# A new hand-written order and a split last copy in an attention and cosine FFN kernel

## The chip, the cores and the metric

The kernel runs on one core of a Trainium2 chip. The metric is the device time of one execution, in microseconds (us); the time of a kernel is the median of several runs.

## The reference

The first half is linear attention with random features on 64 heads (8 batches of 8 heads, 576 positions, 64 values each); its result is laid out as 4608 tokens of 512 values. The second half is a feed-forward layer with 2048 hidden values.

```python
def phi(x):
    proj = np.einsum('bhsd,df->bhsf', x, w_phi)
    proj = proj - np.max(np.abs(proj), axis=-1, keepdims=True)
    return np.concatenate([np.exp(proj), np.exp(-proj)], axis=-1)
q_p, k_p = phi(q), phi(k)
kv = np.einsum('bhsf,bhsd->bhfd', k_p, v)
z = np.sum(k_p, axis=2)
num = np.einsum('bhsf,bhfd->bhsd', q_p, kv)
den = np.einsum('bhsf,bhf->bhs', q_p, z)[..., None] + 1e-06
x = (num / den).transpose(0, 2, 1, 3).reshape(4608, 512)
h = x @ w_in
out = (h * np.cos(h)) @ w_out
```

## The kernel before

The kernel is a list of 3778 steps. Each step (`Step`) belongs to one engine (PE = TensorE, ACT = ScalarE, DVE = VectorE, POOL = GpSimd, SP = the queue that issues the DMAs), holds the function that issues its instructions, and names the steps that it depends on and the buffers that it takes or uses. The functions `attention(u)`, `convert`, `reload` and `visit(v)` make the steps; `plan()` then only walks through the table `ORDER`, a list of all step numbers, and calls each step's function. So `ORDER` sets the order of the instructions on every engine and on SP's queue, and each engine works strictly in that order. `plan()` also gives each buffer of the ring "bank" (the eight PSUM banks) the bank whose last user stands earliest in the table; so a new order gives other banks too. The rings of buffers in SBUF have the sizes in `rings`: three for "eq", two for "o", three each for the weights "wi" and "wo", two for "v".

**Attention.** There are 32 units of two heads each. A unit loads q and k (`load`) and v (`load_v`); PE projects q (`q_mm`, `q_end`) and k (`k_mm`, `k_end`); for the first units PE also subtracts the maximum (`k_sub`). ACT makes the exponentials (`exp_k`, `exp_q`). PE forms the product of keys and values (`kv_mm`: from unit 8 on one step of 72 matmuls, L705 and L711), ACT copies it (`kv_out`), and PE applies the queries (`x_mm`, two steps with 72 matmuls in all, L740 and L746). DVE divides and transposes, and SP stores the unit's result to `xs` in memory. The matmuls of `kv_mm` and `x_mm` have 65 or 130 columns.

**Feed-forward.** The tokens are worked in batches of 512 (`c`), each split into visits (`v`, the list `course`) that go through pairs of weight tiles. The first nine visits (stage "m.") take plain products of 512 columns (`mm1`, L960); the later ones (stage "n.") use a Strassen-like scheme with seven products of six 256-column matmuls each (`mm1`, L912), between which ACT copies partial sums (`snap`, L924) and DVE adds (`even`, `odd`). Then follow cosine and splitting into a high and a low part on ACT and DVE, and the second product, `mm2` (six matmuls of 512 columns, L1009 to L1011; a step `one` is half of it), which adds into four banks `acc`. The weights are converted once (`convert`) and stored in a second form; from the later visits on they are loaded again (`reload`, L516: `wi` 1792 KB, `wo` 1024 KB).

**The end of a visit.** `out_copy` copies the four banks to SBUF: tb 0 and 2 on ACT (L1056), tb 1 and 3 on DVE (L1058), or it adds the earlier partial sum (L1049); `out_store` stores them. The last visit but one is the batch of tail rows (c = 8); its store makes four DMAs for each copy (L1065). In the last visit the copies go to buffers of the ring "eq", which attention no longer needs.

The steps that the text names: 315 and 316 `exp_q`, 321 and 322 `x_mm` of unit 7; 408 `load_v` and 436 `kv_mm` of unit 10; 943 and 1216 `kv_mm` of units 23 and 30; 1554 the last `mm2` of a visit of stage "m.", 1559 and 1561 two of its copies, 1560 and 1562 their stores; 3494, 3498, 3500, 3496 the copies of the tail batch; 3543 to 3546 the first four steps `one` of the last visit; 3650 and 3651 products of that visit; 3776 the last copy, 3777 its store.

Of the kernel before, what the change touches and what calls it, by code (L numbers as in the profile page):

```python
# [25 lines left out]
def phi_attention_then_cos_ffn(ctx: ExitStack, tc: tile.TileContext, qkT, vS, w_phi, w_in, w_out, out):  # L26
# [5 lines left out]
    DM, FF = w_in.shape  # L32
# [35 lines left out]
    class Step:  # L68
# [1073 lines left out]
```

## Time and profile before

| | |
|---|---|
| median of 3 runs | 1047.81 us |
| the runs | 1048.76, 1045.80, 1047.81 us |
| the profiled execution | 1045.83 us |
| its span (first to last instruction) | 1044.1 us |
| what lies around the span | 1.7 us |
| mean granted TensorE clock | 0.998 of 2.4 GHz |

The profile is of one execution. PE is TensorE's matmuls, PEld its weight loads. The ends of matmuls are modelled, so distances are best taken from start to start.

### The profile page before, as it was taken

The numbers are of one execution on the slowest core, as the hardware profiler recorded it, in microseconds if no ns is written. First come the engines' busy times: TensorE is split into PE (matmuls) and PEld (weight loads), VectorE is DVE, ScalarE is ACT, GpSimd is POOL, SyncE is SP. The second block draws the span as 40 slices with busy tenths as digits, with TensorE's granted clock in tenths as the row PEclk, the third lists the DMA queues.
The fourth block names the chain that finished last, engine by engine and source line by source line (L and its number), as shares of the span: only waits on it lengthen the run. The fifth ranks groups of instructions, "written<-read, shape, count | busy, mean of one in ns | idle before, by whom it ended". The sixth has DMA issues, their size and how long they took to land.

```text
span 1044.1 us, 24213 instructions
## 1 busy us (share of the span) xinstructions
PE 1029.5 (99%) x9738; PEld 883.2 (85%) x9738; DVE 744.7 (71%) x1426; ACT 797.6 (76%) x1639; POOL 147.9 (14%) x231
## 2 busy tenths in 40 slices
PE   9998999999999999999999999999999999999998
PEld 6777788888878878888888898989888999898896
DVE  7999898999798877765776467666566465555444
ACT  6989999888887799785788869895887664455443
POOL 3453322201102001301122010211011000000000
PEclk9999999999999999999999999999999999999999
DMA  7576566267556836795427662585435755652852
GB/s 247 178 238 210 161 192 210 85 232 284 173 198 208 284 106 213 245 313 213 161 86 283 202 240 78 171 315 178 160 97 192 255 164 179 245 197 80 277 201 81
DMA packets 88768, 204.44 MB, mean 196 GB/s; under 512 B 20688, under 2 KB 42320, under 8 KB 84816
## 3 DMA queue, kind: packets, MB, share of 16 engines
q1 hardware_dynamic: 88512, 202.83, 57.4%
q8 instruction: 76, 1.25, 0.5%
q14 instruction: 36, 0.29, 0.1%
q10 hardware_dynamic: 144, 0.07, 0.0%
HBM read 154.63 MB, written 48.23 MB: 194 GB/s over the span
## 4 chain that ended last, share of the span: by engine, by line
PE 87%; DMA 6%; DVE 4%; ACT 1%; issue 1%; SPq 0%; DVEq 0%; ACTq 0%
PE bank L912 23%; PE bank L1009 12%; PE bank L1010 12%; PE bank L1011 12%; PE bank L960 10%; PE bank L740 5%; PE bank L705 5%; PE bank L555 3%; PE bank L601 3%; DMA wi_parts<-wi 2%; PE bank L711 1%; DMA wi<-wi_parts 1%; DMA qk<-qkT 1%; PE bank L647 1%; DMA x_raw<-xs 1%
## 5 line engine op out<-in xcount | busy, mean ns | idle before, releaser
L1009 PE MATMUL bank<-wo,gh 128*128 128x512 f32 x576 | 229.1, 398 | 1.1 <-DMA out<-o 0.8
L1010 PE MATMUL bank<-wo,gh 128*128 128x512 f32 x576 | 225.6, 392 | 0.2 <-DVE wo L462 0.2
L1011 PE MATMUL bank<-wo,gl 128*128 128x512 f32 x576 | 224.5, 390 | 0.0
L986 DVE SCALAR_TENSOR_TENSOR g<-g,hs 128x512 f32<-128x512 int32 x144 | 98.5, 691 | 69.2 <-ACT g L982 60.4
L594 POOL TENSOR_TENSOR pq<-pq,bq 128x288 f32<-128x288 f32 x128 | 111.7, 903 | 184.2 <-DVE bq L590 133.3
L924 ACT ACTIVATE hs<-bank 128x256 f32<-128x256 f32 x192 | 71.5, 385 | 86.0 <-PE bank L912 80.7
L659 ACT ACTIVATE ek<-bank,mk 128x128 f32<-128x128 f32 x464 | 128.4, 410 | 3.2 <-DVE mk L642 2.9
L1009 PEld LDWEIGHTS bank<-wo,gh 128*128 128x128 f32 x576 | 108.5, 188 | 24.9 <-issue 2.8
L1011 PEld LDWEIGHTS bank<-wo,gl 128*128 128x128 f32 x576 | 108.2, 188 | 23.7
L49 ACT ACTIVATE gh<-g 128x512 fp32r<-128x512 f32 x144 | 90.9, 637 | 48.4 <-DVE g L993 25.9
L993 DVE TENSOR_TENSOR g<-hs,g 128x512 f32<-128x512 f32 x144 | 99.5, 696 | 38.0 <-ACT g L990 37.5
L54 DVE TENSOR_TENSOR gl<-g,gh 128x512 fp32r<-128x512 f32 x144 | 99.2, 691 | 37.6 <-ACT gh L49 36.2
L912 PE MATMUL bank<-xh_t,wi 128*128 128x256 f32 x768 | 124.4, 284 | 0.0
L1010 PEld LDWEIGHTS bank<-wo,gh 128*128 128x128 f32 x576 | 108.6, 189 | 18.1 <-DVE wo L462 0.7
L990 ACT ACTIVATE g<-g,halfpi 128x512 f32<-128x512 f32 x144 | 101.3, 718 | 23.0 <-DVE g L986 22.4
L912 PEld LDWEIGHTS bank<-xh_t,wi 128*128 128x128 f32 x768 | 109.5, 191 | 7.5 <-ACT hs L924 0.8
L586 POOL COPY m<-m 32x36 f32<-32x36 f32 x96 | 35.5, 369 | 464.5 <-DVE m L581 461.8
L912 PE MATMUL bank<-xh_b,wi 128*128 128x256 f32 x576 | 93.0, 284 | 0.0
L912 PEld LDWEIGHTS bank<-xh_b,wi 128*128 128x128 f32 x576 | 82.4, 191 | 5.4 <-DVE xt L771 0.8
L665 ACT ACTIVATE eq<-pq 128x576 f32<-128x576 f32 x128 | 81.3, 708 | 4.0 <-PE bank L746 2.2
L912 PE MATMUL bank<-xl_t,wi 128*128 128x256 f32 x384 | 77.3, 283 | 0.0
L740 PEld LDWEIGHTS bank<-kv,eq 128*64 128x64 f32 x2048 | 65.5, 139 | 11.2 <-ACT eq L665 3.7
(91 smaller groups left out, 1809.5 us busy)
## 6 DMA issues: line engine op xcount, KB each, us to landing
wi<-wi_parts SPq DMA_DIRECT2D x30, 1792.0 KB, 8.0
wo<-wo_parts SPq DMA_DIRECT2D x30, 1024.0 KB, 5.6
qk<-qkT SPq DMA_DIRECT2D x31, 640.0 KB, 4.8
x_raw<-xs SPq DMA_DIRECT2D x47, 256.0 KB, 4.8
vs<-vS SPq DMA_DIRECT2D x32, 325.0 KB, 4.7
wi_raw<-w_in SPq DMA_DIRECT2D x8, 1024.0 KB, 6.8
wo_raw<-w_out SPq DMA_DIRECT2D x8, 1024.0 KB, 6.7
xs<-xt SPq DMA_DIRECT2D x128, 64.0 KB, 4.5
```

Source lines behind the costliest of these rows:

```text
L54: eng.tensor_tensor(out=out, in0=in_, in1=hi.bitcast(F32), op=ALU.subtract)
L594: qeng.tensor_tensor(out=d["pq"][:, c], in0=d["pq"][:, c], in1=d["bq"][:, c], op=ALU.subtract)
L659: ACT.activation(out=e[:, g, s * P:(s + 1) * P], in_=pk[:, g, :], func=AF.Exp, scale=1.0 - 2.0 * s, bias=d["lk" if s == 0 else "mk", i][:, ...
L740: PE.matmul(out=ps[64 * h:64 * h + 64, 65 * g:65 * g + 65], lhsT=d["eq", j][:, n, c:c + 64], rhs=d["kv"][:, 2 * n + j, :], start=h not in ...
L912: PE.matmul(out=out, lhsT=w[:, part, block, j * P:(j + 1) * P], rhs=d[x, name][:, j * HC:(j + 1) * HC], start=start and k == 0, stop=k == ...
L960: PE.matmul(out=bank(b), lhsT=w[:, part, 2 * r + kt // 2, kt % 2 * P:(kt % 2 + 1) * P], rhs=d.get(("from", kt), d)[x, kt], start=(k == 0), ...
L986: DVE.scalar_tensor_tensor(out=g, in0=g.bitcast(I32), scalar=-TWO_PI, in1=m["hs", r], op0=ALU.mult, op1=ALU.add)
L990: ACT.activation(out=n["g"], in_=n["g"], func=AF.Sin, bias=halfpi, scale=1.0)
L993: DVE.tensor_tensor(out=n["g"], in0=m["hs", r], in1=n["g"], op=ALU.mult)
L1009: PE.matmul(out=a, lhsT=gh[:, t], rhs=w[:, 0, r], start=first, stop=False)
L1010: PE.matmul(out=a, lhsT=gh[:, t], rhs=w[:, 1, r], start=False, stop=False)
L1011: PE.matmul(out=a, lhsT=gl[:, t], rhs=w[:, 0, r], start=False, stop=last)
```

## The change

The table `ORDER` is replaced as a whole; it has one entry more (3779), because the last copy is now two steps. Before the change, TensorE passes from one kind of matmul to another 468 times along the table (grouping `kv_mm` with `x_mm`, `q_end` with `k_end`, and all 512-column steps of the feed-forward part), after it 419 times. The set of steps is otherwise the same. ACT loads its tables of functions 76 times along the old order and 70 times along the new one.

The copy of the last bank (tb = 3 of the last visit, step 3776) goes to a buffer of the ring "o" in place of "eq"; ACT copies its first 256 columns and a new step on DVE (`half_copy`, 3777) the other 256; the store (now 3778) waits for both.

The diff, with the table cut to the lines that hold the steps named above (old lines first):

```diff
     ORDER = [
...
-        1533, 397, 524, 411, 1523, 1569, 1534, 1542, 379, 1326, 361, 425, 1566, 381, 408, 427, 360, 1293, 383,
...
-        462, 1576, 422, 1562, 447, 448, 434, 421, 464, 366, 466, 436, 450, 1329, 451, 1330, 1555, 400, 1577,
...
-        943, 965, 908, 909, 2476, 2501, 2486, 910, 2525, 911, 2505, 2524, 2477, 2527, 2487, 2450, 2530, 944,
...
-        1232, 1179, 1244, 1231, 1234, 1216, 1233, 3001, 1235, 2991, 1181, 1236, 1182, 3040, 1183, 1246, 3013,
...
-        3598, 3573, 3620, 3581, 3599, 3622, 3545, 3500, 3600, 3617, 3574, 3625, 3621, 3546, 3575, 3609, 3496,
...
-        3766, 3767, 3770, 3768, 3772, 3771, 3769, 3774, 3775, 3773, 3776, 3777,
...
+        316, 285, 339, 1316, 315, 1541, 1317, 392, 1318, 370, 1319, 1522, 371, 372, 321, 389, 446, 391, 1523,
...
+        1576, 462, 1561, 450, 502, 451, 466, 1562, 449, 1586, 408, 1577, 328, 467, 418, 366, 1578, 452, 1555,
+        421, 454, 1332, 1344, 400, 1557, 524, 419, 367, 1587, 464, 420, 399, 1311, 453, 422, 436, 507, 1333,
...
+        909, 967, 2475, 943, 966, 973, 2476, 968, 2505, 2486, 2477, 2447, 2506, 944, 954, 2525, 874, 2526, 2448,
...
+        3038, 3021, 2991, 1146, 3022, 1179, 2992, 3023, 1216, 3043, 1233, 3024, 1247, 1181, 3003, 1235, 2993,
...
+        3593, 3580, 3499, 3543, 3597, 3599, 3581, 3544, 3600, 3617, 3601, 3545, 3574, 3546, 3575, 3553, 3582,
...
+        3765, 3759, 3766, 3767, 3770, 3768, 3772, 3771, 3769, 3774, 3773, 3776, 3775, 3777, 3778,
     ]
...
-                if v == len(course) - 1:
+                if v == len(course) - 1 and tb < NB3 - 1:
                     o = d["o", tb] = new("eq", [P, 2, S], F32, "o_last")[:, 0, 0:DM]
                 else:
                     o = d["o", tb] = new("o", [P, DM], F32, "o")
-                if tb % 2 == 0:
+                if v == len(course) - 1 and tb == NB3 - 1:
+                    ACT.activation(out=o[:, 0:HC], in_=bank(acc[tb])[:, 0:HC], func=AF.Copy, scale=1.0)
+                elif tb % 2 == 0:
                     ACT.activation(out=o, in_=bank(acc[tb]), func=AF.Copy, scale=1.0)
                 else:
                     DVE.tensor_copy(out=o, in_=bank(acc[tb]))
...
-            o = Buf("o" if v < len(course) - 1 else "eq")
-            eng = "ACT" if fresh and tb % 2 == 0 else "DVE"
+            def half_copy(tb=tb):
+                DVE.tensor_copy(out=d["o", tb][:, HC:DM], in_=bank(acc[tb])[:, HC:DM])
+
+            very_last = v == len(course) - 1 and tb == NB3 - 1
+            o = Buf("o" if v < len(course) - 1 or very_last else "eq")
+            eng = "ACT" if fresh and tb % 2 == 0 or very_last else "DVE"
...
-            cp = Step(eng, 0.5 if eng == "ACT" else 0.61, out_copy, [done[tb] if v == len(course) - 1 else before] + old, take=[] if old else [o],
+            cp = Step(eng, (0.27 if very_last else 0.5) if eng == "ACT" else 0.61, out_copy, [done[tb] if v == len(course) - 1 else before] + old, take=[] if old else [o],
                       use=[acc[tb]] + ([o] if old else []), kind=stage + "out_copy")
-            partial[c, tb] = Step("SP", 0.36 if c < TAIL else 1.5, out_store, [cp], use=[o], kind=stage + "out_store", pipe=0.75)
+            cps = [cp]
+            if very_last:
+                cps.append(Step("DVE", 0.34, half_copy, [done[tb]], use=[acc[tb], o], kind=stage + "out_copy"))
+            partial[c, tb] = Step("SP", 0.36 if c < TAIL else 1.5, out_store, cps, use=[o], kind=stage + "out_store", pipe=0.75)
```

## Rows read from the trace of the kernel before

**Rows 1.** The page's first part: busy us (share of the span) xinstructions of each engine.

```profile
PE 1029.5 (99%) x9738; PEld 883.2 (85%) x9738; DVE 744.7 (71%) x1426; ACT 797.6 (76%) x1639; POOL 147.9 (14%) x231
```

**Rows 2.** Busy time by stretch; behind the engines: granted clock, DMA share, GB/s.

```profile
93.00:97.00 4.00, 1.49 (x10) 0.50 (x8) 3.90 (x10) 3.97 (x6) 0.92 (x4) 1.00 0.95 298
97.00:101.00 4.00, 3.80 (x70) 3.68 (x70) 3.90 (x10) 4.00 (x14) 0.21 (x1) 0.61 0.86 307
101.00:112.00 11.00, 10.29 (x180) 8.26 (x179) 10.70 (x21) 11.00 (x27) 5.37 (x10) 0.99 0.73 193
...
566.00:573.00 7.00, 5.94 (x152) 5.43 (x152) 4.11 (x12) 5.26 (x13) 3.07 (x4) 1.00 1.02 397
573.00:779.00 206.00, 206.00 (x2037) 181.53 (x2037) 128.14 (x269) 165.59 (x365) 25.37 (x42) 1.00 0.52 176
779.00:785.00 6.00, 4.41 (x131) 4.04 (x127) 5.74 (x17) 5.94 (x10) 0.62 (x3) 1.00 0.99 354
...
971.00:976.00 5.00, 4.23 (x30) 3.76 (x29) 2.97 (x6) 2.71 (x6) 0.00 (x0) 1.00 0.53 143
...
1039.60:1044.10 4.50, 0.00 (x0) 0.00 (x0) 0.69 (x1) 0.00 (x0) 0.00 (x0) 0.92 0.49 186
```

**Rows 3.** Who PE waited for: us in total, times, longest.

```profile
PE bank L711 <- issue: 2.6, 2, 1.6
```

**Rows 4.** Timeline of PE around 1020 us: start, duration, engine, line.

```profile
1020.23 0.64 PE L912 MATMUL bank<-xh_b,wi 128*128 128x256 f32 x4
...
1020.95 0.40 PE L1009 MATMUL bank<-wo,gh 128*128 128x512 f32 x1
...
1022.34 0.39 PE L1009 MATMUL bank<-wo,gh 128*128 128x512 f32 x1
...
1023.70 0.64 PE L912 MATMUL bank<-xh_t,wi 128*128 128x256 f32 x4
...
1024.41 0.40 PE L1009 MATMUL bank<-wo,gh 128*128 128x512 f32 x1
```

**Rows 5.** Timeline of PE, 780 to 785 us.

```profile
782.36 0.61 PE L711 MATMUL bank<-vs,ek 128*64 128x130 f32 x7
784.55 0.33 PE L711 MATMUL bank<-vs,ek 128*64 128x130 f32 x1 [1.59 <-issue]
```

**Rows 6.** The page's DMA queues: packets, MB, share of 16 engines.

```profile
q8 instruction: 76, 1.25, 0.5%
```

**Rows 7.** Busy time and counts from the start to each of the two waits.

```profile
0.00:570.45 570.45, 563.77 (x5827) 467.69 (x5827) 471.02 (x902) 488.11 (x987) 118.81 (x182) 1.00 0.61 205
0.00:782.70 782.70, 774.97 (x7991) 653.99 (x7991) 604.70 (x1183) 658.22 (x1359) 144.54 (x226) 1.00 0.59 199
```

**Rows 8.** Timeline, 965 to 975 us, the end of the tail batch.

```profile
965.45 0.58 ACT L1056 ACTIVATE o<-bank 128x512 f32<-128x512 f32 x1
966.05 7.21 SPq L1065 DMA_DIRECT2D out<-o  x8
...
973.76 0.69 DVE L1058 COPY o<-bank 128x512 f32<-128x512 f32 x1 [1.94 <-DMA out<-o]
...
974.50 0.50 PE L1009 MATMUL bank<-wo,gh 128*128 128x512 f32 x1 [0.77 <-DMA out<-o]
```

**Rows 9.** Timeline behind 1038 us.

```profile
1039.17 0.39 PE L1011 MATMUL bank<-wo,gl 128*128 128x512 f32 x1
...
1040.33 0.69 DVE L1058 COPY o_last<-bank 128x512 f32<-128x512 f32 x1 [1.40 <-DMA out<-o_last]
```

**Rows 10.** Groups by line: count, busy us, mean ns, idle before.

```profile
L924 ACT ACTIVATE hs<-bank 128x256 f32<-128x256 f32 x192 | 71.5, 385 | 86.0 <-PE bank L912 80.7 <-DVE g L993 4.2
...
L943 DVE TENSOR_TENSOR hs<-bank,hs 128x256 f32<-128x256 f32 x48 | 20.1, 419 | 55.0 <-PE bank L912 53.4 <-ACT hs L924 1.4
```

**Rows 11.** Weight loads of L516: from issue to landing.

```profile
DMA to landing us min/median/max: 4.8/7.6/11.5
```

**Rows 12.** The page's DMA issues: queue, count, KB each, median us from issue to landing.

```profile
vs<-vS SPq DMA_DIRECT2D x32, 325.0 KB, 4.7
```

409 rows, old and new, of the table ORDER are left out of this document.

## The prediction

> **What bounds the kernel now.** I read the page's busy line first [rows 1], then the busy time of every engine stretch by stretch [rows 2], then who made TensorE (PE) wait [rows 3], and last the timeline at each place where PE stood idle. The busy line shows PE at 99%: 1029.5 of 1044.1 us, so 14.6 us of idle PE is about all that a better order can win, beside what PE loses while it is busy. The stretches show where that idle time lies. From 185 us on the other engines are no limit (in 573 to 779 us ScalarE (ACT) has 165.6 and VectorE (DVE) 128.1 busy of 206), and PE is idle in only a few places: 1.06 us in 566 to 573, 1.59 in 779 to 785, 0.77 in 971 to 976, and 4.5 us behind the last matmul [rows 2]. Before that, in 93 to 112 us, it is idle 2.51 + 0.20 + 0.71 = 3.4 us, and there ACT is busy 3.97 of 4, 4.00 of 4 and 11.00 of 11: ACT sets the pace, not the order of PE. In 97 to 101 us the granted clock is 0.61, that is, part of it went at the lower level (1.2 GHz), after the 2.5 us without matmuls. As matmul ends are modelled, I take PE's costs from start to start, not from its busy time.
>
> **Width changes.** Along the table PE goes from 256-column products (mm1 of the later visits, L912) to 512-column matmuls (mm2, one) 107 times before and 81 times after; all changes among matmul kinds fall from 468 to 419, but those that are not between 256 and 512 columns are 246 in both. A step of six 512-column matmuls lasts 1022.34 - 1020.95 = 1.39 us behind a product and 1023.70 - 1022.34 = 1.36 behind its own kind; a product lasts 1020.95 - 1020.23 = 0.72 behind a product and 1024.41 - 1023.70 = 0.71 behind a 512 step [rows 4]. So 26 fewer entries at 0.03 save 0.8 us, and 23 fewer returns at 0.01 give 0.2 back: **-0.5 us** (between 0 and -0.8, the rows being round to 0.01). The other 246 changes I take at nothing, since their number stays.
>
> **The two waits inside attention's last matmuls.** Both stand at L711, in kv_mm of units 23 and 30 (steps 943, 1216), and are put down to "issue": 2.6 us in two [rows 3]. From start to start the second costs more than its idle time: a run of seven started at 782.36, and the eighth came at 784.55 instead of about 782.75, some 1.8 us late [rows 5]; the first, 1.06 idle, I put at 1.3 in the same way, so 3.1 together. Nothing in the data flow was late there, but instructions were: the instruction queue brought 76 packets with 1.25 MB [rows 6], that is 16.4 KB each, and PE's 2 x 9738 instructions [rows 1] are 256 to a packet. The two waits come in front of matmul 5827 and 7991 [rows 7]; the 4328 instructions between are 17 x 256 less 24, and PE's stream holds event instructions too, which no count here includes. Both fell in a run of 144 matmuls (x_mm, x_mm, kv_mm back to back), which passes 256 instructions in under 4 us, and while the DMA engines were full (share 1.02 and 0.99, against 0.52 in between) [rows 2]. So a packet comes late where a long run of short matmuls, a packet's border and a big weight load meet. The new table breaks the run of step 943 (in front of it stand 512- and 256-column steps and k_mm) and keeps that of step 1216. Runs of 128 matmuls and more are 18 before and 17 after; counted with the border where it fell before, no run after 185 us in the new one ends on a border with a weight load just ahead, but a dozen more or fewer event instructions would put one there. I take -3.1 plus 0.7 for a new one: **-2.4 us** (between -3.1 and 0). The Trainium skill ("Runtime: NRT & Kernel Launch", Instruction fetch mechanics) says that PE is refilled in 16 KiB blocks of 256 instructions, as the packets here show, and that crossing a border is mostly hidden; these two waits disagree. By that rule alone the waits would be something else and stay, and the sum would be 2.4 us smaller (rival 2).
>
> **The end of the tail batch.** The visit before the last stores its result in pieces: step 3494's copy starts at 965.45, eight stores take SP's queue from 966.05 on, the third copy (3500) waits 1.94 us for a buffer and starts at 973.76, and PE's first matmul into that copy's bank (step 3546) at 974.50, held 0.77 us [rows 8]. From copy to that matmul it is 974.50 - 965.45 = 9.05 us. In the old table only 6.4 us of PE work stood between steps 3543 and 3546. In the new one 3546 takes another bank; the banks of the two late copies go to products 3650 and 3651, and between 3543 (now the first behind 3494's copy) and 3650 stand four "one" steps (half an mm2 each), five products and three mm2: 4 x 0.68 + 5 x 0.72 + 3 x 1.37 = 10.4 us, over 9.05. **-0.8 us** (between 0 and -1.0).
>
> **The last copy.** The last matmul starts at 1039.17 and its bank could be read at about 1039.6, but the copy starts at 1040.33, after 1.40 us, because its buffer ("eq", three of them) must first be stored by the first of the four stores [rows 9]; it ends at 1041.02, and the store, SP's last issue and the end follow (4.5 us without PE in all). In the new kernel the buffer is one of ring "o", last used by the visit before, so nothing holds it. No row shows ScalarE and VectorE reading one bank at once; the nearest are 128x256 reads of a bank alone, 0.385 us on ACT and 0.419 on DVE [rows 10]. Side by side the copy ends at 1039.6 + 0.42 = 1040.0, one after the other at 1040.4: **-1.0 us** (between -0.6 and -1.0; I take the first, as the two steps name no wait on each other). The Trainium skill ("PSUM — Partial Sum Buffer", PSUM bank collisions raise a hardware error) wants two engines kept apart on one bank, reads included; with such a wait added the gain would be the 0.6.
>
> **The early stretch.** In front of the first x_mm of unit 7 (steps 321 and 322), where PE waited longest, ACT has the same 96 steps ahead of exp_q 315 in both tables, and PE 97 steps in both, of which two differ. With ACT full [rows 2], that wait stays: **0** (gain up to 3.4 us idle and 1 us of slow clock, loss up to 1). One load moves the wrong way: v of unit 10 (step 408) stood ahead of the two partial stores 1560 and 1562 in SP's queue and now stands behind them, so it waits for their copies, and the stores, weight load and x loads queued behind it wait as well. Cover: 10.3 us of PE work stand between the last mm2 ahead of these copies (step 1554) and kv_mm of unit 10 (436); the load takes 4.7 us [rows 12], the copy some 0.7 of its own and what is queued on DVE. It costs nothing unless the copy comes over 5 us late. Six fewer table loads on ACT cost and win nothing, as ACT waits for others after 185 us.
>
> **The sum** is -0.5 - 2.4 - 0.8 - 1.0 = -4.7 us. The profiled execution took 1045.83 us, the fastest but one of those shown, and the median is 1047.81. From the first it gives 1041.1, from the second 1043.1; I take the middle, 1042.1.
>
> **Rivals.** (1) The early waits go as well, because fewer matmuls that need ACT stand ahead of the ones that do not: for it speaks that PE steps which wait for ACT and DVE stand a little later behind their sources in the new table; against it the full ACT. All 3.4 us idle plus 1 us of clock: about 1038. (2) The change does not do what it says: the waits for instructions only move, since runs of short matmuls are as many as before. Then -2.3 is left: 1044.5, and a second hit in 1044 to 1047. (3) Slower: weight reloads come late. A wi load takes 4.8 to 11.5 us, median 7.6 [rows 11]. PE work between a load's place and its first product is least with 8.4, 9.1, 9.8 and 10.3 us in the new table (four products and four mm2 are 4 x 0.72 + 4 x 1.37 = 8.4), against 9.8, 9.9, 10.4 and 10.5 before, and the old trace shows no PE wait for such a load. If these four all landed after 11.5 us they would cost 3.1 + 2.4 + 1.7 + 1.2 = 8.4 us, and the kernel would end at about 1050; it is slower than before once they land after about 10.6 on the mean, and slower by over 0.3% after 11.4.
>
> **Chances.** About 0.3% (3.1 us, below 1044.7) is what a measurement of this kernel can tell from no change. The forecast holds with 0.53 (its own range 1039.5 to 1044.5), rival 1 with 0.15, rival 2 with 0.22, rival 3 with 0.06, and 0.04 is left for several small new waits. Faster is nearly all of the forecast, rival 1 and a third of rival 2, whose time lies at the bound: 0.73; within 0.3% the rest of rival 2 and part of what is left: 0.19; slower, rival 3 and the rest: 0.08. Rival 1's far end and rival 2 lie inside 1037 to 1047.5, which leaves out under 2 in 10.
>
> **What would show it.** In the new profile: two L711 rows without "issue", or one elsewhere in a run of short matmuls (rival 2); no wait of L1009 for the store of o near 970 us; a last copy in two rows of about 0.4 us that start 0.1 us or less behind the last matmul's end; the idle time in 93 to 112 us as before (if it halves, rival 1); PE waits put down to wi (rival 3), or kv_mm of unit 10 waiting for vs. The prediction is wrong if the early idle time moves by over 2 us, or if new idle time of over 2 us appears after 185 us.

## The result and the profile after

The changed kernel takes 1037.65 us (median of 4 runs, 1037.56 to 1039.34), the kernel before 1048.04 (4 runs): a ratio of 0.9908 with a 95% interval of 0.989 to 0.9926, that is 7.8 to 11.5 us less. A repeat beside the last experiments (E11) gave 0.9914 (0.9901 to 0.9927). The two profiled executions differ by less, 8.2 us (spans 1044.1 and 1035.9); why the medians differ by more is part of what follows. The forecast of 1042.1 had the direction and held the time in its outer range (1037 to 1047.5), but the time lies below the forecast's own range (1039.5 to 1044.5): it stood 5.7 us under the median of before known then, and the measured gain is 10.4 us.

The page's busy line of after, the answer to [rows 1]: TensorE (PE) has 9.5 us without work instead of 14.6.

```profile
PE 1026.4 (99%) x9738; PEld 883.3 (85%) x9738; DVE 742.9 (72%) x1426; ACT 790.0 (76%) x1634; POOL 147.7 (14%) x231
```

Who PE waited for, in after (us in total, times, longest; "issue" stands where nothing that the profile shows held PE up). The L711 row of [rows 3] is gone, and so is the wait of [rows 8] for a store of `o`; the long wait in front of unit 7's x_mm (L740; 2.5 us in before) is still there.

```profile
PE bank L740 <- ACT ek L659: 2.7, 1, 2.7
PE bank L1098 <- DVE warm L355: 1.1, 1, 1.1
PE bank L705 <- ACT pq L566: 0.5, 1, 0.5
PE bank L912 <- issue: 0.4, 1, 0.4
PE bank L558 <- ACT kv L717: 0.3, 1, 0.3
```

Busy time by stretch in after (as [rows 2]). PE is full in 566 to 573, 779 to 785 and 971 to 976 us, where it lost 3.4 us before, although the DMA engines are as full there, and in 971 to 976 us fuller (1.00 against 0.53).

```profile
54.00:80.00 26.00, 26.00 (x451) 20.98 (x447) 25.06 (x60) 24.89 (x67) 10.87 (x16) 1.00 0.66 196
93.00:112.00 19.00, 15.81 (x244) 11.96 (x245) 17.11 (x35) 18.22 (x50) 5.37 (x10) 0.91 0.78 266
566.00:573.00 7.00, 7.00 (x68) 6.19 (x63) 4.24 (x11) 6.94 (x19) 0.23 (x1) 1.00 1.04 402
779.00:785.00 6.00, 6.00 (x156) 5.83 (x152) 5.06 (x16) 4.56 (x10) 1.05 (x3) 1.00 0.98 399
971.00:976.00 5.00, 5.00 (x40) 4.84 (x39) 2.40 (x5) 1.63 (x3) 0.00 (x0) 1.00 1.00 376
```

The first two stretches in before: 93 to 112 us is as it was (3.4 us idle, now 3.2), but 54 to 80 us lost 1.2 us that after does not lose.

```profile
54.00:80.00 26.00, 24.82 (x477) 20.31 (x472) 24.81 (x55) 23.21 (x59) 11.40 (x16) 1.00 0.76 237
93.00:112.00 19.00, 15.58 (x258) 12.44 (x256) 18.50 (x39) 18.97 (x44) 6.50 (x14) 0.91 0.80 239
```

The end of after, the answer to [rows 9]. The copy's first half starts 0.43 us behind the last matmul's start, with no wait for a buffer. The second half starts only when the first has ended, and its releaser is the first half.

```profile
1031.59 0.39 PE L1011 MATMUL bank<-wo,gl 128*128 128x512 f32 x1
1032.02 0.38 ACT L1056 ACTIVATE o<-bank 128x256 f32<-128x256 f32 x1
1032.43 0.42 DVE L1072 COPY o<-bank 128x256 f32<-128x256 f32 x1 [1.08 <-ACT o L1056]
1032.88 0.33 SPq L1069 DMA_DIRECT2D out<-o  x1
```

**Where the 8.2 us went.** I gave each kind of step and each change of kind a clean cost, the time it takes where PE waits for nothing (fitted to PE's starts in both traces; this is a calculation), and call the rest waiting. Us beyond the clean cost, by stretch of time:

```
kernel   clean cost  to 56  -93  -112  -176  -560  -585  -760  -800  -960  to the last matmul
before      1018.0    0.6   2.7   6.0   0.6   2.0   1.5   0.4   1.9   0.1   1.1
after       1017.4    0.6   0.8   6.0   0.6   1.5   0.0   0.3   0.1   0.1   0.1
```

The differences are: clean cost -0.6, the two L711 waits -3.3, the tail batch -1.0, 56 to 93 us -1.9, the stretches left over -0.7; the copy behind the last matmul ends 1.26 us after that matmul's start instead of 1.85, -0.6. The sum is -8.1.

### The profile page after: what moved, and what is told of

Its sections match the earlier page's. It is cut to its first block, busy times and chain, and to the rows that moved or that the text cites. A ratio compares the mean times of both kernels' runs of the same rounds, so it can differ in the third digit from the quotient of the medians.

```text
span 1035.9 us, 24223 instructions
## 1 busy us (share of the span) xinstructions
PE 1026.4 (99%) x9738; PEld 883.3 (85%) x9738; DVE 742.9 (72%) x1426; ACT 790.0 (76%) x1634; POOL 147.7 (14%) x231
## 4 chain that ended last, share of the span: by engine, by line
PE 95%; DVE 3%; issue 1%; DMA 0%; SPq 0%; ACT 0%; DVEq 0%
PE bank L912 23%; PE bank L1009 13%; PE bank L1010 12%; PE bank L1011 12%; PE bank L960 12%; PE bank L705 6%; PE bank L740 6%; PE bank L555 3%; PE bank L601 3%; PE bank L711 1%; PE bank L647 1%; PE bank L558 1%; PE bank L626 1%; PE bank L746 1%; DMA wo_parts<-wo 0%
## 5 line engine op out<-in xcount | busy, mean ns | idle before, releaser
L1009 PE MATMUL bank<-wo,gh 128*128 128x512 f32 x576 | 229.5, 399 | 0.0
L594 POOL TENSOR_TENSOR pq<-pq,bq 128x288 f32<-128x288 f32 x128 | 114.2, 923 | 172.1 <-DVE bq L590 121.5
L1009 PEld LDWEIGHTS bank<-wo,gh 128*128 128x128 f32 x576 | 108.4, 188 | 23.3 <-issue 2.2
L912 PE MATMUL bank<-xh_t,wi 128*128 128x256 f32 x768 | 124.0, 284 | 0.4 <-issue 0.4
L912 PEld LDWEIGHTS bank<-xh_t,wi 128*128 128x128 f32 x768 | 109.4, 191 | 6.4 <-issue 1.2
L586 POOL COPY m<-m 32x36 f32<-32x36 f32 x96 | 32.7, 341 | 469.4 <-DVE m L581 445.4
L912 PE MATMUL bank<-xh_b,wi 128*128 128x256 f32 x576 | 93.3, 284 | 0.0
L912 PEld LDWEIGHTS bank<-xh_b,wi 128*128 128x128 f32 x576 | 81.0, 191 | 2.8 <-issue 0.2
L982 ACT ACTIVATE g<-hs 128x512 int32<-128x512 f32 x96 | 60.2, 638 | 24.5 <-DVE hs L939 18.9
L912 PE MATMUL bank<-xl_t,wi 128*128 128x256 f32 x384 | 77.3, 283 | 0.0
```

The costliest lines, as they stand in the source:

```text
L594: qeng.tensor_tensor(out=d["pq"][:, c], in0=d["pq"][:, c], in1=d["bq"][:, c], op=ALU.subtract)
L912: PE.matmul(out=out, lhsT=w[:, part, block, j * P:(j + 1) * P], rhs=d[x, name][:, j * HC:(j + 1) * HC], start=start and k == 0, stop=k == ...
L1009: PE.matmul(out=a, lhsT=gh[:, t], rhs=w[:, 0, r], start=first, stop=False)
```

## The experiments

Each ran beside the kernel before on one chip, E1 to E4, E5 to E8 and E9 to E12 together. Ratios are to the kernel before in the same set. Where the table was rewritten, the line numbers are 22 lower than in before or after: L718 is L740, L689 is L711, L890 is L912, L987 is L1009 of before.

**E1, the last copy alone**, in the old table. The diff is after's own, with the old `ORDER` ending in 3776, 3777, 3778.

> The old table with only the last copy changed (a buffer of ring o, columns 0 to 255 on ScalarE, 256 to 511 on VectorE). After's profile shows the second half starting 0.03 us behind the end of the first. If the halves follow one another because the second waits for the first, they do so here too: the span is 0.6 us shorter than before's 1044.1, 1043.5, and the second half waits for o of L1056. If they stand one behind the other only by the end of the new table, they run side by side here and the span is 1043.1.

Ratio 1.000 (0.999 to 1.0011), span 1043.6. The halves follow one another here too; from the last matmul's start to the end of the copy it is 1.26 us, as in after. By the copy's place the gain is the 0.6, not the 1.0; the timed runs, uncertain by 1 us, cannot tell the two from each other or from nothing. That the span agrees is partly luck: PE waited 0.4 us less than in before, and from the copy to the end it took 3.52 us instead of after's 3.08.

```profile
1038.79 0.39 PE L989 MATMUL bank<-wo,gl 128*128 128x512 f32 x1
1039.22 0.38 ACT L1034 ACTIVATE o<-bank 128x256 f32<-128x256 f32 x1
1039.63 0.42 DVE L1050 COPY o<-bank 128x256 f32<-128x256 f32 x1 [1.08 <-ACT o L1034]
```

**E2, the last copy whole**, on ACT, in after's table:

```diff
-                if v == len(course) - 1 and tb == NB3 - 1:
-                    ACT.activation(out=o[:, 0:HC], in_=bank(acc[tb])[:, 0:HC], func=AF.Copy, scale=1.0)
-                elif tb % 2 == 0:
+                if tb % 2 == 0 or v == len(course) - 1 and tb == NB3 - 1:
                     ACT.activation(out=o, in_=bank(acc[tb]), func=AF.Copy, scale=1.0)
```

> After's table with the last copy in one piece on ScalarE, into the buffer of ring o. The 128x512 copies on ScalarE take 0.60 us in after's tail, the two halves 0.38 + 0.03 + 0.42 = 0.83. If the halves run one after the other, the whole copy is 0.23 us faster: a span of 1035.7 against 1035.9. If splitting gained anything, the span grows by up to 0.2.

The copy ends 1.02 us behind the last matmul's start, 0.24 sooner than the two halves. The span (1036.8; ratio 0.9919, 0.9905 to 0.9932) does not show it: this execution waited 1.0 us more elsewhere, and in 56 to 93 us alone 1.2 more, with after's table.

```profile
1032.59 0.39 PE L989 MATMUL bank<-wo,gl 128*128 128x512 f32 x1
1033.01 0.60 ACT L1034 ACTIVATE o<-bank 128x512 f32<-128x512 f32 x1
```

**E9, the halves in two buffers:**

```diff
+                d["o2", tb] = new("o", [P, DM], F32, "o2")
-                DVE.tensor_copy(out=d["o", tb][:, HC:DM], in_=bank(acc[tb])[:, HC:DM])
+                DVE.tensor_copy(out=d["o2", tb][:, HC:DM], in_=bank(acc[tb])[:, HC:DM])
```

> After's kernel with the two halves of the last copy in two buffers of ring o, each with a store of its own. If the second half waited for the first because both write one buffer, the halves now run side by side: the VectorE half starts within 0.1 us of the ScalarE half, the copies end 0.4 us earlier behind the last matmul than after's 1.26 us, and the span falls by 0.1 to 0.4 us from 1035.9. If the common bank is what orders them, the VectorE half starts behind the end of the ScalarE half here too and the copies end as in after.

They still follow one another, so it is not the shared buffer; what the two still share is the bank. Ratio 0.9909 (0.9894 to 0.9925), as after.

```profile
1033.98 0.38 ACT L1034 ACTIVATE o<-bank 128x256 f32<-128x256 f32 x1
...
1034.39 0.42 DVE L1051 COPY o<-bank 128x256 f32<-128x256 f32 x1 [1.08 <-ACT o L1034]
```

**E3, the borders moved by 84 instructions,** in before:

```diff
-        for _ in range(WARM):
+        for _ in range(4):
             PE.matmul(out=banks[7][:, 0:P], lhsT=warm, rhs=warm, start=True, stop=True, skip_group_check=True)
+        for _ in range(24):
+            PE.matmul(out=banks[7][0:16, 0:16], lhsT=warm[:, 0:16], rhs=warm[:, 0:16], start=True, stop=True, skip_group_check=True)
```

> Before with another warm-up: 4 products of 128 columns and 24 of 16 columns in place of 7 of 128 columns, so that 84 more instructions of TensorE (42 matmuls with their weight loads) stand ahead of everything else. Each border of 256 instructions then falls 42 matmuls earlier in the table, which is otherwise before's. Theory (instructions come late where a border closes a block that lies whole in a run of short matmuls, with full DMA engines): neither L711 row waits for issue, and the span is some 3.1 to 3.4 us under before's, about 1040.9, give or take what the warm-up itself changes at the start (up to 1 us). Rival (the waits come from the weight loads or from a dependence that the profile does not name, and hang on the place in the table): both waits stay, 2.6 us in all, and the span is that of before within 1 us.

Ratio 0.9961 (0.9949 to 0.9974), 4.1 us less, with the old table. No L711 row is left among the waits of PE; the wait at the tail batch is, longer than in before.

```profile
PE bank L740 <- DVE xt L771: 2.5, 1, 2.5
PE bank L1009 <- DVE o L1058: 1.6, 1, 1.6
...
PE bank L912 <- issue: 0.4, 1, 0.4
```

**E5, the borders moved by 16:** the same with `range(6)` and `range(5)`.

> Before with 6 warm-up products of 128 columns and 5 of 16 columns in place of 7 of 128, so that 16 more instructions of TensorE stand ahead of everything else and each border of 256 instructions falls 8 matmuls earlier. Theory (late instructions at the borders): both waits follow the border, from in front of the last or last but one of the eight L711 matmuls into the end of the 64 L705 matmuls of steps 943 and 1216, some 0.3 us earlier in the run; together 2 to 3.5 us, and the span stays within 1 us of before's 1044.1. Rival (fixed to the place in the table): they stay in front of the last L711 matmuls. If a small shift is enough to end them, neither wait is there and the span is near 1041.

Ratio 0.9962 (0.9947 to 0.9976), span 1040.6: moving the border by 8 matmuls ends both waits, the third case. Three small waits for issue are left, at 27.8, 68.6 and 443.0 us:

```profile
PE bank L740 <- issue: 0.7, 2, 0.5
...
PE bank L705 <- issue: 0.3, 1, 0.3
```

**E6, after with its borders moved by 180:** `range(2)` and `range(50)` in after's kernel.

> After's kernel with its whole order, and a warm-up of 2 products of 128 and 50 of 16 columns in place of 7 of 128: 180 more instructions of TensorE ahead, and a first product some 0.8 us later. Counted in after's trace, borders then close blocks inside runs of short matmuls at 783 and at 679 us, with DMA shares of 0.99 and 0.86 in the 5 us before. Theory (after was rid of the waits because its borders fall elsewhere): waits for issue of 1 to 2 us near 783 and 0.3 to 1.3 us near 679, and a span of 1035.9 + 0.8 + 2.3 = 1039.0. Rival (the new order itself has no such wait, since it broke the run of step 943): no wait for issue above 0.5 us, and a span of 1036.7.

Ratio 0.9945 (0.9932 to 0.9958): 3 to 4 us of after's gain are gone, 0.6 of them in the longer warm-up. In the profile the wait is back in step 1216, in the new table; at 679 us there is none. The span, 1037.5, is after's plus 0.6 for the warm-up and 1.6 for this wait, less 0.7 in smaller ones.

```profile
782.58 0.61 PE L711 MATMUL bank<-vs,ek 128*64 128x130 f32 x7
784.53 0.27 PE L711 MATMUL bank<-vs,ek 128*64 128x130 f32 x1 [1.34 <-issue]
```

**E12, one weight load later:** in the old table 2521 stands behind 913 instead of ahead of 939.

> Before with one change: the weight load 2521, which SP issues at 565.50 us and whose first user starts at 601 us, stands behind store 913 (578.5 us). Borders and runs of matmuls stay as they were. If a packet of instructions is late because it queues behind the weight load just issued, the packet for the block that ends in step 943 starts about 1.1 us behind its border instead of 2.8, the L711 wait at 571.8 us is gone, the one at 784.5 us stays (1.6 to 1.9), and the span is 1.2 to 1.5 us under before's, about 1042.7. If the run of short matmuls at a border is enough: both waits stay, 2.6 us, and the span is 1044.

The expectation holds in part. The packet starts 2.0 us behind its border instead of the 1.1 expected, and the first wait shrinks from 1.2 us to 0.3; from 567 to 570 us the DMA engines are still 0.96 busy, with loads issued before. The second wait, untouched, is 3.2 us in this execution, so the waits are no shorter in sum (span 1045.7), and the ratio is 1.0001 (0.9989 to 1.0013).

```profile
567.00:570.00 3.00, 3.00 (x94) 2.73 (x94) 0.55 (x4) 2.98 (x10) 2.72 (x4) 1.00 0.96 356
```

```profile
571.29 1.17 PE L689 MATMUL bank<-vs,ek 128*64 128x130 f32 x8
...
786.18 0.33 PE L689 MATMUL bank<-vs,ek 128*64 128x130 f32 x1 [2.93 <-issue]
```

With matmuls, weight loads and the semaphore instructions of PE's queue numbered in the order of their starts, all nine such waits in these kernels come in front of a matmul with number 193 or 194 modulo 256. I call that place a border; the table has the time of the border before, 256 numbers earlier, and the packet of the instruction queue that came in between (counted from the traces; us):

```
kernel  step  border before  packet starts, ends  PE goes on  wait
before   943      566.56       569.36  570.29       571.77     1.2
before  1216      778.86       782.38  783.34       784.55     1.9
E1       943      566.46       568.71  569.64       571.18     0.7
E1      1216      778.27       781.57  782.53       783.82     1.7
E4       943      568.29       570.70  571.60       573.18     1.1
E4      1216      780.16       783.57  784.51       785.85     1.7
E6      1216      779.08       782.13  783.09       784.53     1.6
E12      943      567.74       569.73  570.72       572.02     0.3
E12     1216      779.14       783.76  784.69       786.18     3.2
E5       943      565.55       566.77  567.82       no wait at the border, 569.34
E5      1216      776.42       777.51  778.46       no wait at the border, 780.15
after    943      559.38       563.03  563.95       no wait at the border, 566.20
```

PE goes on 1.2 to 1.6 us after the packet's end every time. The wait grows with the packet's delay behind the border before: 2.0 us gives 0.3, 2.8 gives 1.2, 3.5 gives 1.9, 4.6 gives 3.2. In E5 the border comes 1 to 2.4 us sooner, the packet starts after 1.2 and 1.1 us, and PE waits for nothing. In after the packet is 3.65 us late, but 6.8 us of PE's work lie between the two borders, where a run of short matmuls has about 4 (5.2 less the wait of 1.2 in before).

The weight loads do not tell E5 from before: the same two are issued 0.8 and 2.1 us ahead of the border before in E5, 1.1 and 2.4 us in before. The DMA engines are full behind them in E5 too. In before:

```profile
565.50 0.52 SPq L516 DMA_DIRECT2D wi<-wi_parts  x1
...
776.49 0.52 SPq L516 DMA_DIRECT2D wi<-wi_parts  x1
```

In E5, with the stretches behind the two borders before:

```profile
564.73 0.52 SPq L516 DMA_DIRECT2D wi<-wi_parts  x1
...
774.29 0.52 SPq L516 DMA_DIRECT2D wi<-wi_parts  x1
```

```profile
565.00:567.00 2.00, 2.00 (x58) 1.68 (x58) 0.35 (x2) 2.00 (x9) 1.67 (x3) 1.00 1.06 372
...
777.00:779.00 2.00, 2.00 (x76) 2.00 (x74) 1.88 (x4) 1.98 (x5) 0.00 (x0) 1.00 0.94 359
```

The smaller waits for issue in the lists above (three in E5, one each in after, E3 and E8: 0.3 to 0.5 us) have the same numbers, and PE goes on 1.2 to 1.5 us after the packet's end there too. Those of after, E3 and E8 stand in front of a product (L912), with 5.9 to 7.1 us from border to border, the wait included; in after that packet started 4.85 us behind the border before. So a run of short matmuls is not needed: it is where the work between two borders is least, and a late packet costs most. In before the same border, the 37th, falls into a step of 16 k_mm matmuls at 484.3 us, which takes 1.47 us instead of the 1.0 to 1.1 of its like behind 400 us. In after, then in before:

```profile
481.53 0.74 PE L912 MATMUL bank<-xh_t,wi 128*128 128x256 f32 x4 [0.38 <-issue]
```

```profile
484.29 1.54 PE L601 MATMUL bank<-wphi,qk 64*128 64x128 f32 x16
485.76 0.50 PE L912 MATMUL bank<-xh_t,wi 128*128 128x256 f32 x2
```

**E4, the new table up to 79 us** (its first 356 steps, the rest in the old order).

> Before's kernel with the first 356 steps of the new table and behind them all other steps in the old order (the sets of the two tables differ there by 12 steps, none of them TensorE's). If the early gain of after is made by the order between 56 and 80 us (three waits of k_end 305, k_mm 345 and kv_mm 317, 1.9 us), TensorE's idle time up to 80 us falls to about that of after and the span is about 2.0 us shorter, 1042.1, with both L711 waits and the 2.5 to 2.8 us wait at x_mm of unit 7 still there. If ScalarE's full load only hands the time on to the next wait, the time returns by 112 us and the span stays at 1044.

Ratio 0.9999 (0.999 to 1.0008), span 1045.1. The seam spoils it: a q_end waits 1.6 us and x_mm of unit 7 3.0 instead of 2.5, and the early part loses 12.3 us up to 176 us, more than either table. It tells nothing of the early order in after.

```profile
PE bank L718 <- DVE rb L745: 3.0, 1, 3.0
PE bank L536 <- ACT pq L544: 1.6, 1, 1.6
```

**E7, the early part new** (892 steps, to 214 us, with E3's warm-up).

> The old table with its first 892 steps taken from the new one (up to about 214 us, where both have issued the same matmuls), the rest in the old order, and the warm-up with 84 more instructions that took both L711 waits away (alone: span 1041.6, median 1042.56 us). In the traces so far the part up to 176 us waits 9.8 to 10.3 us beyond TensorE's clean cost with the old table and 8.0 to 8.3 with the new. If the new order of that part is worth it: 1.8 us of waits and 0.4 of width changes less, a span of 1039.4 and a median of 1040.4. If the seam at 214 us or ScalarE takes it back, as at the seam at 79 us: 1041.6 and 1042.6.

Ratio 0.9962 (0.995 to 0.9975) against E3's 0.9961: nothing gained. In its profile a k_mm waits 1.4 us until 34.08, where after has no wait with the same steps. The row names the DVE copy that ends then, but in after the same k_mm runs ahead of that copy; what is late is its load of q and k, issued at 25.16 and landed 8.8 us later, where the loads of that time took 4.5 and 6.3 in after.

```profile
PE bank L579 <- DVE xt L749: 1.4, 1, 1.4
```

**E10, the early part old,** the rest after's.

> After's kernel with the first 892 steps (up to about 214 us) in the old order and the rest of the new table. If the new order of the early part is worth what the two profiles show (9.9 us of waits up to 176 us with the old, 8.0 with the new), the span is 1035.9 + 1.9 + 0.2 = 1038.0 and the median about 2 us over that of after's repeat in the same set. If that difference is only the luck of single executions, as the opposite exchange had it (1043.2 against 1042.6): the median is within 0.7 us of after's.

Ratio 0.9957 (0.9945 to 0.9969), 4.4 us over E11. But 2.9 us of that execution's waits stand between 176 and 300 us, just behind the seam, where after has 0.3:

```profile
237.50 0.96 PE L938 MATMUL bank<-xh_b,wi 128*128 128x512 f32 x3 [1.35 <-ACT o L1036]
```

Taken from the 4.4, that leaves some 1.8 us for the early part and the width changes in it; this is an estimate, since the profiled execution was the slowest of the six. By the fitted clean cost, waits up to 176 us are 9.9, 10.3, 9.8, 9.9, 8.3, 10.4 and 11.1 us with the old early part (before, E1, E3, E5, E8, E10, E12), mean 10.0; with the new one 8.0, 8.3, 7.8, 10.0, 10.1 and 9.0 (after, E2, E6, E7, E9, E11), mean 8.9. The new order gains about 1 us there by this count, less than one execution differs from the next, so it is not shown clear of noise.

**E8, the late part new** (from step 3487, about 940 us, with the new last copy and E3's warm-up).

> The old table up to its step 3487 (about 940 us) and the new one from there, with the new last copy and the warm-up with 84 more instructions (alone: span 1041.6, median 1042.56 us). The wait at the tail batch was 0.9 to 1.7 us in the four kernels with the old end (1.7 in that one) and none with the new; the last copy ends 0.6 us earlier. Both together: a span of 1039.2 to 1040.1, a median of 1040.2 to 1041.1, and no wait of L1009 for o near 970 us. If the stores of the tail batch only hand the wait on to the products that take the two banks in the new order: a wait of about 1 us at an L912 there, and 1041.

Ratio 0.9928 (0.9915 to 0.9941), by the medians 3.3 us under E3, more than the 1.5 to 2.4 expected. The span is 4.3 us shorter: 1.8 at the tail batch, 0.6 at the last copy, 0.2 of clean cost, and 1.6 less waiting up to 176 us, where the two kernels are the same. Why the timed runs gain 1 us over the two parts stays open. E8 has the old order up to 940 us and still comes within 1.5 us of after (0.9928 against E11's 0.9914; spans of 1037.3 against 1035.9 and 1037.2). So most of after's gain is had with the old order up to 940 us, by borders that fall elsewhere and by the new end. What the new order does besides, before 940 us, is worth 1.5 us or so, which is not clear of noise. No wait of mm2 for `o` is left, and none at the products that take the two banks; at the front of the list:

```profile
PE bank L718 <- DVE xt L749: 2.5, 1, 2.5
...
PE bank L890 <- issue: 0.3, 1, 0.3
```

**E11, after again.**

> After's kernel again, beside the three others: a median of 1037.6 within 0.7 us, a spread of under 2 us between its runs, and no wait for issue above 0.6 us.

Median 1038.41 (1037.31 to 1039.30), no wait for issue; 0.1 above the expected bound.

## Why the prediction was right, and where it was not

**Width changes**, -0.5 forecast: the fitted clean cost falls by 0.6. The size agrees; no run changes the widths alone.

**The two waits in attention's last matmuls**, -2.4 forecast: the mechanism was right, the size too small. Both are late instructions at a border of 256: E3 and E5 end them with the old table, E6 brings one back with the new. The term was mis-sized twice. The 0.7 set aside for a new wait was not needed (the one of 0.5 us at 481.5 us in after comes at a border that costs before some 0.4, at 484.7 us in another step). And the profiled execution's 3.1 to 3.3 are not what the waits cost in the mean: single waits at step 1216 run from 1.6 to 3.2 us in the profiles, and the medians of E3 and E5 lie 4.1 and 4.4 us under before's. That is also why the medians differ by more than the profiled executions: before's 49 runs in the three sets spread over 4.4 us (1044.64 to 1049.01), the 9 of E3 and E5 over 1.5. One reason given for it was wrong: breaking the run of step 943 does not make the new table safe. It keeps the run of step 1216 and is safe there by where its borders fall, and 180 instructions undo that. Rival 2, by which the waits only move, did not come, but nothing in the order excludes it. That a weight load makes the packet late, the third part of the mechanism forecast, is not shown. E12's first wait speaks for it, but 0.3 us were left and the timed runs show no gain; E5 speaks against it: the same loads are issued as close ahead of the border before, the DMA engines are full behind both, and the packets start after 1.2 and 1.1 us. The Trainium skill ("Runtime: NRT & Kernel Launch", Instruction fetch mechanics) calls the crossing mostly hidden; of the 76 packets in before two held PE up by over 1 us and a third by some 0.4, and those two cost more than any other part of the change gained.

**The tail batch**, -0.8 forecast: -1.0 in the profile. In the seven profiles with the old end the wait is 0.9 to 1.7 us, mean 1.2; it depends on when the eight stores land. The count of PE work between the copy and its bank's next user was the right argument: no wait is left in E8 or after.

**The last copy**, -1.0 forecast, -0.6 measured. The step that failed is "Side by side the copy ends at 1039.6 + 0.42 = 1040.0, one after the other at 1040.4", of which I took the first because "the two steps name no wait on each other". The table names none, but the program has one: in E1, after and E9 the VectorE half starts 0.03 us behind the end of the ScalarE half, with one buffer or two. The Trainium skill ("PSUM — Partial Sum Buffer", PSUM bank collisions raise a hardware error) says that the compiler's scheduler orders two engines on one bank, reads included; the runs agree, and the other bound was the term. Split this way the copy is slower than whole (0.83 against 0.60 us, E2): the gain comes from the buffer alone. It is 0.6 us by the profiles and too small for the timed runs to show.

**The early stretch**, 0 forecast. The claim itself held: in 93 to 112 us PE waits 6.0 us beyond its clean cost in both. What failed is that I took that stretch for all that could change early. In 56 to 93 us, where ScalarE's order differs and a 512-column step (1517) now stands ahead of kv_mm 317, 1.9 us of waits (k_mm 345, kv_mm 317, k_end 305) are gone in the profiled execution; over the profiles the mean up to 176 us falls by about 1. Which of the moved steps does it stays open, since tables joined in the early part wait at the seam (E4, E10). Rival 1 named this time (1038) but another place and reason, and did not happen; that its time came out is luck.

**The load moved the wrong way** (408) cost nothing, nor did the weight loads of rival 3: PE waits for neither `vs` nor `wi` in after, though a weight load took up to 13.2 us (11.5 before). That six table loads fewer were worth anything is not shown by any run.

## What to carry to other kernels

A wait of TensorE for "issue" is worth numbering, in a long run of short matmuls above all: if it falls on the same number modulo 256 each time, some instructions more or fewer ahead of it can end it with the order unchanged (E3, E5), and any later edit can bring it back (E6). A cost read from one profiled execution is one draw; where waits hang on when a DMA lands, the difference between medians can be 2 us larger than that between two profiles. In every profile here with the split copy, the two engines that read halves of one PSUM bank did not share the time: one read after the other.

## What the runs showed that I had not expected

Sixteen instructions in the warm-up of a kernel of about 19,570 numbered ones were worth 4.4 us (E5), nearly half of what the whole change gained, and with the new end added (E8, with E3's warm-up) all but some 1.5 us of it. A border 8 matmuls earlier left nothing of the 1.2 and 1.9 us, since the packets then started 1.1 to 1.2 us behind the border before instead of 2.8 to 3.5; what makes them start that much sooner is not shown. Neither a weight load nor full DMA engines tell the two cases apart.
